# A gated linear attention with a mixture of eight experts: first unit's decay in two interleaved halves, expert rows gathered ahead of weights, range verdict moved into the last expert

## The chip, the cores and the metric

The kernel runs on one core of a Trainium2 chip. The metric is the device time of one execution in microseconds, the median of three runs. A core has a matrix engine (PE, with its weight loads shown apart as PEld), a vector engine (DVE), a scalar engine (ACT), a general-purpose engine (POOL) and a queue engine (SP) that here only starts transfers. Each engine works through its own list of instructions in the order in which they stand there. A profile of one execution gives every instruction with its start, its length and what released it.

## What is computed

The reference has two blocks. The first is a gated linear recurrence with a complex decay for each channel, for 4 batches, 8 heads, 768 steps and 48 channels a head; its output is regrouped into 3072 rows of 384. The second sends every row to the one of eight experts that has the largest logit, and scales the result by the softmax weight of that expert.

```python
mag = np.sqrt(a_re * a_re + a_im * a_im)
scale = np.minimum(mag, 0.999) / (mag + 1e-06)
a_re_n, a_im_n = (a_re * scale, a_im * scale)
for t in range(S):
    new_re = ar * S_re - ai * S_im
    new_im = ar * S_im + ai * S_re
    S_re, S_im = (new_re + kv, new_im)          # kv: outer product of k and v at t
    y[:, :, t] = np.einsum('bhd,bhde->bhe', q[:, :, t], S_re)
...
expert_idx = np.argmax(x @ w_gate, axis=1)
for e in range(E):
    h = np.maximum(x_sorted[lo:hi] @ w1[e], 0.0)
    y_sorted[lo:hi] = h @ w2[e]
return gate_w[:, None] * y
```

## The kernel before

**Attention stage.** The recurrence is computed in chunks of 128 steps. There are 24 chunks (6 blocks of time by 4 batches), and two of them, of two neighbouring batches, make a unit: 12 units, u = 0 to 11, with tiles of 128 partitions by 768 columns (`W`). For each unit SP loads ar and ai (the real and imaginary decay), q, k and v, of 384 KB each (`load`, line 257). The tiles ar, q and k have two buffers, ai and v three. Then:

- `decay_steps` (277) makes the logarithm of the decay's size, in the tile A, and the tangent of its angle, in ai. ACT and DVE alternate: Ln of ar; Exp, DVE product with ai (289), Square; Ln, DVE add (294); Exp, DVE minimum and subtract (299). R holds what passes from one to the other.
- `decay_angle` (303) makes the angle by Arctan on ACT, for which another table of functions has to be loaded, and later units pass the angle at the end of their time block on by small transfers that POOL starts (309, 318, with a DVE addition in c at 315).
- `decay_sums` (327) and `angle_sums` (356) are prefix sums over the 128 steps by products with a triangular matrix on PE (csl for the size, cst for the angle), then Exp on ACT (E and Ei) and a reduction to one turn on DVE.
- `rotation` (379) makes cosine and sine; `decayed` (387) and `rotated` (395) multiply them into q and k, which gives the tiles Q and K.
- `scores` (481) transposes Q and K on PE (tp), copies them out (qt, kt), multiplies them (at) and masks the result on DVE (am); dk is the chunk's contribution to the state. `outputs` (510) adds the two parts of y, updates the state G, transposes y back and computes the routing logits.

The loop over u (587) works on the decay of unit u + 1, on the angles of unit u, and on scores and outputs of unit u - 1. A scheduler puts the instructions of each engine into order when the kernel is built, so an edit in one place can move instructions elsewhere; some are tied to one another by `queue`, which all ACT functions of the decay are. `busy` (248) puts idle products of the identity matrix with itself on PE at the start, whose results nobody reads: 30 before the first sums and 28 after those of the first unit.

**Routing and experts.** `choose` and `route` find each row's expert and place; POOL scatters the rows with an indirect transfer to the DRAM tile `xs`, where each expert has 448 places. `gather` (550) loads the rows of one expert, in an order of experts that is computed on the chip, in four copies to the tile sq (two buffers) and one or two small ones to gi (gate and row number). `turn` (671) transposes sq to xt by DVE in three instructions, `expert` (704) forms hps = w1 times xt, in eight groups of three products, with relu to ht in turns on DVE and ACT, and then yps = ht times w2, whose tiles of 128 rows DVE scales by the gate to y and POOL scatters to the output. The first expert is done in two parts, of 256 and 192 rows. Its second part gathers its rows after the attention stage; then come `load_w(1)` and, at the start of that part (811), the gather of the second expert. Weights have two sets of buffers, so those of expert e + 2 are loaded behind expert e (824).

**Range check.** The fast formulas hold for decays within a range. From the second to the seventh expert, ACT and POOL check two of twelve slices of ar and ai each (`range_check`, 760, between hps and yps of the expert), and leave sums in `bad`. `verdict` (779) adds them up on DVE, lets PE sum over partitions (`bp`, 798), and writes the flag that decides, at the end of the kernel, if slower code has to be run. It stands after the seventh expert (829). With the inputs here, the flag is zero and the slow code isn't run.

Of the kernel before, what the change touches and what calls it, by code (L numbers as in the profile page):

```python
# [10 lines left out]
FP = mybir.dt.float32  # L11
# [3 lines left out]
OP = mybir.AluOpType  # L15
# [5 lines left out]
P = 128  # L21
# [16 lines left out]
def kernel(  # L38
# [189 lines left out]
    def act(**kw):  # L228

        ins = nc.scalar.activation(**kw)  # L230
        if "act" in T:
            queue(ins, T["act"])
        T["act"] = ins
# [20 lines left out]
                queue(w, m)  # L254
            m = w

    def load(u, names):
        for nm, src in names:
            if nm == "v":
                t = vbuf[u % 3][:, :, :, 0:D]  # L260
                T[nm, u] = vbuf[u % 3]
            else:
                t = ld.tile([P, U, H, D], FP, tag=nm, name=nm, bufs=3 if nm == "ai" else 2)
                T[nm, u] = t.rearrange("p c h d -> p (c h d)")
            s, b = divmod(u * U, B)
            T["ld"] = nc.sync.dma_start(
                out=t.rearrange("p c h d -> p (c h) d"),
                in_=src[b : b + U, :, s * P : (s + 1) * P, :].rearrange("b h t d -> t (b h) d"),
            )

    def load_a(u):
        load(u, (("ar", a_re), ("ai", a_im)))
# [1 line left out]
    def load_qkv(u):  # L274
        load(u, (("q", q), ("k", k), ("v", v)))

    def decay_steps(u):

        ar, ai = T["ar", u], T["ai", u]
        A = un.tile([P, W], FP, tag="A", name="A")  # L280
        R = un.tile([P, W], FP, tag="R", name="R", bufs=1)
        T["L", u], T["th", u] = A, ai

        def s0():
            act(out=A, in_=ar, func=AF.Ln)

        def s1():
            act(out=R, in_=A, func=AF.Exp, scale=-1.0)
            nc.vector.tensor_tensor(out=ai, in0=ai, in1=R, op=OP.mult)
            act(out=R, in_=ai, func=AF.Square)  # L290

        def s2():
            act(out=R, in_=R, func=AF.Ln, bias=1.0)
            nc.vector.scalar_tensor_tensor(out=A, in0=A, scalar=2.0, in1=R, op0=OP.mult, op1=OP.add)

        def s3():

            act(out=R, in_=A, func=AF.Exp, scale=-0.5, bias=ln2e6)
            nc.vector.scalar_tensor_tensor(out=A, in0=A, scalar=LN_CAP2, in1=R, op0=OP.min, op1=OP.subtract)

        return [s0, s1, s2, s3]

    def decay_angle(u):

# [51 lines left out]
    def angle_sums(u, c):  # L356

        if c == 0:
            for nm in ("f", "fa"):
                T[nm, u] = un.tile([P, W], FP, tag=nm, name=nm, bufs=1)  # L360
        sl = slice(c * DM, (c + 1) * DM)
        f = T["f", u][:, sl]
        cs = sums("cst", u, c)
        m = mm(cs, tri_turn, T["th", u][:, sl])
        if u == 0 and c == 1:
            busy(m, 28)
        r = ch.tile([P, DM], FP, tag="r", name="r")
        nc.vector.tensor_scalar(out=r, in0=cs, scalar1=MAGIC, scalar2=MAGIC, op0=OP.add, op1=OP.subtract)
        nc.vector.tensor_tensor(out=f, in0=cs, in1=r, op=OP.subtract)
        if c == U - 1:  # L370
            f, fa = T["f", u], T["fa", u]
            nc.vector.tensor_scalar(
                out=fa.bitcast(I32), in0=f.bitcast(I32), scalar1=0x7FFFFFFF, scalar2=None, op0=OP.bitwise_and
            )
            if (u + 1) * U <= NT - B:
                T["fl", u] = un.tile([96, 8], FP, tag="fl", name="fl", bufs=3)
                nc.gpsimd.dma_start(out=T["fl", u], in_=f[P - 1 : P].rearrange("o (p j) -> o p j", j=8))
# [172 lines left out]
    def gather(e, s, sizes):  # L550

        n, w = len(sizes), sum(sizes)
        f, nb = w // P, -(-w // TB)
        sq = gp.tile([P, nb, KD * TB], FP, tag="sq", padded_shape=[P, CAP // TB, KD * TB], name="sq")
        gi = gp.tile([P, n, 2], FP, tag="gi", padded_shape=[P, CT, 2], name="gi", bufs=3)
        rows = xs[0:NS].rearrange("(e s) c -> e s c", s=CAP)[ds(ex[e], 1), s : s + nb * TB]
        for a in range(QB):  # L560
            x = rows[:, :, a * KD * TB : (a + 1) * KD * TB]
            nc.sync.dma_start(out=sq[a * TB : (a + 1) * TB], in_=x.rearrange("o (b j) c -> j (o b) c", j=TB))
        nc.sync.dma_start(out=gi[:, :f], in_=rows[:, : f * P, DM:].rearrange("o (i p) c -> p (o i) c", p=P))
        if f < n:
            nc.sync.dma_start(out=gi[0 : w - f * P, f], in_=rows[:, f * P : w, DM:].rearrange("o p c -> (o p) c"))
        return sq, gi

    load_a(0)
    load_qkv(0)
    for z in range(2):  # L570
        nc.sync.dma_start(
            out=wg[z * DP : z * DP + D, :, 0:E],
            in_=w_gate.rearrange("(i z d) e -> z d i e", z=2, d=D)[z],
        )
    load_a(1)
    busy(None, 30)
    table("natural_log_exp_and_others")
    for f in decay_steps(0):
        f()
    table("trig_and_small")  # L580
    decay_angle(0)
# [5 lines left out]
    for u in range(NU + 1):  # L587
        if 0 < u < NU:
            load_qkv(u)
        for i in range(NS // (P * BL)):  # L590
            if 2 + i * 2 // (NS // (P * BL)) == u:
                blank(i)

        if u < NU:
            steps = decay_steps(u + 1) if u + 1 < NU else []
            own = [lambda c=c: decay_sums(u, c) for c in range(U)]
            steps = steps[:1] + (own + steps[1:] if u == 0 else own[:1] + steps[1:2] + own[1:] + steps[2:])
            table("natural_log_exp_and_others")
            for i, f in enumerate(steps):
                f()  # L600
                if i == 1:
                    carry_angle(u)
            for f in T.pop("chosen", []):
                f()
            for c in range(U):
                angle_sums(u, c)
            table("trig_and_small")
            rotation(u)
            if u + 1 < NU:
                decay_angle(u + 1)  # L610
            if u == NU - 1:
                while T["put"]:
                    place()
                experts_at(range(1), True)
                load_w(0, range(KD + KF // 2))
                own0 = gather(0, 0, [P] * (FIRST // P))
        if u < NU:
            place()
        for f in T.pop("route", []):
            T["put"] += f()  # L620
        for c in range(U):
            g = (u - 1) * U + c
            if g >= 0:
                scores(g)
            if u < NU:
                decayed(u, c)
            if g > 0:
                outputs(g - 1)

            n = {NT - GR: GR, NT - U: U}.get(g)  # L630
            if n:
                if n == GR:
                    queue(table("natural_log_exp_and_others"), T["copied"])
                choose(g - n, n)()
                T["put"] += route(g - n, n)
                while T["put"]:
                    place()
        for _ in range(2 if u >= NU - 2 else 1):
            place()
        if u > 2 and u % 2 and u < NU - 1:  # L640

            j = (u - 3) * U
            T["chosen"] = [choose(j, GR)]
            T["route"] = [lambda j=j: route(j, GR)]
        if u + 2 < NU:
            load_a(u + 2)
# [10 lines left out]
    def tiles(n):  # L657
        return [P] * (n // P) + [n % P] * (n % P > 0)

    rest0 = gather(0, FIRST, tiles(CAPS[0] - FIRST))  # L660
    experts_at(range(1, E), False)
    load_w(1)
    xp = ctx.enter_context(tc.tile_pool(name="xp", bufs=2))
    hp = ctx.enter_context(tc.tile_pool(name="hp", bufs=2))
# [134 lines left out]
        nc.vector.tensor_copy(out=flag, in_=bp)  # L799

    flag = const([1, 2], "flag", I32)
    parts = [(0, [P] * (FIRST // P), own0), (0, tiles(CAPS[0] - FIRST), rest0)]
    xt = turn(parts[0][1], own0[0])
    for e in range(E):
        if e in (1, E - 1):
# [1 line left out]
            T["drain"] = queue(nc.gpsimd.drain(), T["out"])  # L807
        while parts and parts[0][0] == e:
            sizes, (sq, gi) = parts.pop(0)[1:]
            if not parts and e + 1 < E:  # L810
                parts.append((e + 1, tiles(CAPS[e + 1]), gather(e + 1, 0, tiles(CAPS[e + 1]))))
            last = not parts or parts[0][0] > e
            todo = []
            if last and 1 <= e < E - 1:
                todo = [lambda b, i=i: range_check(i, b) for i in range(NC) if i % (E - 2) == e - 1]

            def ahead():
                if parts:
                    T["xt"] = turn(parts[0][1], parts[0][2][0])

            expert(sizes, xt, *W_T[e], gi, todo, ahead)
            xt = T["xt"]
        if e + 2 < E:
            load_w(e + 2)
        for i in range(NC):
            if i % (E - 2) == e:
                range_load(i)
        if e == E - 2:
            verdict()


    TS = 16
# [85 lines left out]
    def others():  # L918
        with tc.tile_pool(name="mo", bufs=1) as mo:
# [8 lines left out]
            with tc.For_i(0, E, 1) as ev:  # L928
# [8 lines left out]
                with tc.For_i(0, NT, 1) as jv:  # L937
                    nc.vector.tensor_copy(out=fi, in_=fr[:, ds(jv, 1)])
                    xg = gp.tile([P, XW], FP, tag="sq", padded_shape=[P, KD * CAP], name="xg")
                    gi = gp.tile([P, 1, 2], FP, tag="gi", padded_shape=[P, CT, 2], name="gi", bufs=3)  # L940
                    nc.gpsimd.indirect_dma_start(
                        out=xg,
                        out_offset=None,
# [42 lines left out]
```

## Time and profile before

| what | value |
| --- | --- |
| median of 3 runs | 563.52 us (563.12 to 565.4) |
| span of the profiled execution | 561.2 us |
| PE busy | 530.6 us, 95% |
| DVE busy | 271.4 us, 48% |
| ACT busy | 278.0 us, 50% |
| POOL busy | 130.2 us, 23% |
| first transpose of Q on PE | at 27.81 us |
| first product of an expert | at 283.51 us |
| moved by DMA | 79.32 MB |

The span is a little shorter than the measured time, which holds the start and end of the program too. A busy PE is not one at its peak: the lengths of its instructions overlap, and its clock can be lower than full, which the profile gives as granted clock (1.00 is full, 0.50 half). In a timeline each line has the start and the length in us, the engine, the line of the kernel, the operation, the tiles written and read, and, where the engine stood idle before the instruction, for how long and what released it. Idle time of an engine costs nothing unless PE waits for that engine in the end.

### The profile page before, as it was taken

The numbers are of one execution on the slowest core, as the hardware profiler recorded it, in microseconds if no ns is written. First come the engines' busy times: TensorE is split into PE (matmuls) and PEld (weight loads), VectorE is DVE, ScalarE is ACT, GpSimd is POOL, SyncE is SP. The second block draws the span as 40 slices with busy tenths as digits, with TensorE's granted clock in tenths as the row PEclk, the third lists the DMA queues.
The fourth block names the chain that finished last, engine by engine and source line by source line (L and its number), as shares of the span: only waits on it lengthen the run. The fifth ranks groups of instructions, "written<-read, shape, count | busy, mean of one in ns | idle before, by whom it ended". The sixth has DMA issues, their size and how long they took to land.

```text
span 561.2 us, 8750 instructions
## 1 busy us (share of the span) xinstructions
PE 530.6 (95%) x3294; PEld 367.8 (66%) x3294; DVE 271.4 (48%) x637; ACT 278.0 (50%) x468; POOL 130.2 (23%) x148
## 2 busy tenths in 40 slices
PE   6699999989999999999999899999999999999895
PEld 6587677768778778777776545555555555565462
DVE  2567788688888888878442122112222131210310
ACT  5777967857787687745310105326152341616100
POOL 2101111131141140210221003406143250604201
PEclk9879999989999999999999999999999999999998
DMA  9999995937575543460117893373945718390001
GB/s 158 182 220 260 246 158 66 171 83 119 108 140 95 107 93 58 98 231 12 48 60 234 231 266 127 110 204 130 280 133 178 231 48 263 126 293 15 26 2 42
DMA packets 163534, 79.32 MB, mean 141 GB/s; under 512 B 144864, under 2 KB 156829, under 8 KB 162587
## 3 DMA queue, kind: packets, MB, share of 16 engines
q1 hardware_dynamic: 158619, 69.04, 53.8%
q0 software_dynamic: 4864, 9.63, 5.1%
q8 instruction: 28, 0.46, 0.3%
q14 instruction: 23, 0.19, 0.1%
HBM read 63.30 MB, written 15.46 MB: 140 GB/s over the span
## 4 chain that ended last, share of the span: by engine, by line
PE 73%; ACT 3%; DVE 3%; issue 2%; DMA 2%; POOL 1%; POOLq 0%; DVEq 0%; ACTq 0%
PE hps L81 24%; PE yps L81 21%; PE y L81 7%; PE at L81 6%; PE tp L492 5%; PE dk L81 3%; PE csl L81 2%; PE cst L81 2%; PE tpx L542 2%; DMA c<-ai 2%; PE lt L81 1%; ACT L242 1%; PE lp L81 1%; POOL cai L774 1%; POOL cs L771 1%
## 5 line engine op out<-in xcount | busy, mean ns | idle before, releaser
L81 PE MATMUL hps<-xt,w1t 128*128 128x256 f32 (+8 forms) x432 | 133.9, 469 | 2.3 <-DVE xt L679 2.3
L81 PE MATMUL yps<-w2t,ht 128*128 128x384 f32 (+6 forms) x464 | 135.0, 487 | 0.0
L81 PEld LDWEIGHTS hps<-xt,w1t 128*128 128x128 f32 x432 | 80.0, 190 | 54.3 <-issue 24.8
L81 PEld LDWEIGHTS yps<-w2t,ht 128*128 128x128 f32 (+6 forms) x464 | 75.9, 177 | 57.0 <-issue 7.1
L713 ACT ACTIVATE ht<-hps 128x256 f32<-128x256 f32 (+8 forms) x36 | 17.0, 472 | 132.2 <-PE hps L81 131.3
L730 DVE TENSOR_SCALAR y<-yps,gi 128x384 f32<-128x384 f32 (+2 forms) x24 | 14.8, 616 | 106.6 <-PE yps L81 106.6
L717 DVE TENSOR_SCALAR ht<-hps 128x256 f32<-128x256 f32 (+8 forms) x36 | 19.2, 533 | 83.6 <-PE hps L81 83.5
L81 PE MATMUL at<-qt,kt 96*128 96x128 f32 x384 | 54.9, 284 | 3.4 <-DVE kt L84 2.7
L81 PEld LDWEIGHTS at<-qt,kt 96*128 96x128 f32 x384 | 49.2, 195 | 10.4 <-DVE kt L84 3.2
L81 PE MATMUL y<-am,v 128*64 128x128 f32 x384 | 51.0, 286 | 0.6 <-DVE am L500 0.5
L693 POOL DMA_INDIRECT out_dram<-y,gi x29 | 28.2, 972 | 93.0 <-DVE y L730 42.8
L470 POOL DMA_INDIRECT xs<-x,slot x24 | 26.2, 1090 | 89.2 <-DMA xs<-x,slot 29.1
L81 PE MATMUL y<-qt,G 96*64 96x128 f32 x320 | 46.0, 281 | 0.7 <-DVE G L537 0.7
L771 POOL TENSOR_TENSOR cs<-cs,cw 128x768 f32<-128x768 f32 x12 | 21.7, 1807 | 87.1 <-ACT cw L767 87.1
L500 DVE TENSOR_TENSOR am<-at,tri 128x512 f32<-128x512 f32 x48 | 33.0, 687 | 14.7 <-PE at L81 14.6
L81 PEld LDWEIGHTS y<-am,v 128*64 128x64 f32 x384 | 33.1, 137 | 9.6 <-issue 8.0
L492 PE MATMUL tp<-ident,Q 128*96 128x128 f32 x192 | 33.5, 285 | 2.1 <-DVE Q L398 1.7
L81 PEld LDWEIGHTS y<-qt,G 96*64 96x64 f32 x320 | 32.6, 137 | 4.4 <-issue 2.7
L242 ACT ACT_TABLE_LOAD x27 | 34.6, 1283 | 1.2 <-PEq L972 0.8
L84 ACT COPY qt<-tp 96x512 f32<-96x512 f32 x48 | 27.8, 581 | 14.0 <-PE tp L492 13.9
L81 PEld LDWEIGHTS dk<-v,K 128*96 128x96 f32 x320 | 31.1, 170 | 3.2 <-issue 1.1
L81 PE MATMUL dk<-v,K 128*96 128x48 f32 x320 | 31.7, 252 | 0.8 <-DVE t L530 0.8
(140 smaller groups left out, 745.9 us busy)
## 6 DMA issues: line engine op xcount, KB each, us to landing
w1t<-in_moe_w_dram SPq DMA_DIRECT2D x7, 1536.0 KB, 6.6
w2t<-in_moe_w_dram SPq DMA_DIRECT2D x7, 1536.0 KB, 7.2
xs<-zrow SPq DMA_DIRECT2D x7, 772.0 KB, 8.7
ar<-in_a_re_dram SPq DMA_DIRECT2D x12, 384.0 KB, 5.9
ai<-in_a_im_dram SPq DMA_DIRECT2D x12, 384.0 KB, 6.6
q<-in_q_dram SPq DMA_DIRECT2D x12, 384.0 KB, 5.8
k<-in_k_dram SPq DMA_DIRECT2D x12, 384.0 KB, 6.2
v<-in_v_dram SPq DMA_DIRECT2D x12, 384.0 KB, 5.1
```

Source lines behind the costliest of these rows:

```text
L81: return nc.tensor.matmul(o, lhsT=lhsT, rhs=rhs, start=start, stop=stop, skip_group_check=True)
L84: (nc.scalar.copy if i % 2 else nc.vector.tensor_copy)(out=o, in_=in_)
L242: ins = nc.scalar.preload_act_table_set(name)
L470: pool(nc.gpsimd.indirect_dma_start(out=xs[:, :], out_offset=bass.IndirectOffsetOnAxis(ap=to[:, i : i + 1], axis=0), in_=x[:, i], in_offse ...
L492: nc.tensor.transpose(out=tp[0:DD, j], in_=X[:, hg * 4 + j], identity=ident)
L500: nc.vector.tensor_tensor(out=am, in0=at, in1=bc(tri, 1, 4), op=OP.mult)
L542: nc.tensor.transpose(out=tp[:, i].rearrange("p z d -> p (z d)"), in_=xt[:, i], identity=ident)
L693: T["out"] = nc.gpsimd.indirect_dma_start(out=out, out_offset=bass.IndirectOffsetOnAxis(ap=idx, axis=0), in_=y[0:m], in_offset=None, bound ...
L713: relu = nc.scalar.activation(out=ht[:, f], in_=ps, func=AF.Relu)
L717: nc.vector.tensor_scalar(out=ht[:, f], in0=ps, scalar1=0.0, scalar2=None, op0=OP.max)
L730: nc.vector.tensor_scalar(out=y[0:m], in0=ps[0:m], scalar1=gate, scalar2=None, op0=OP.mult)
L771: nc.gpsimd.tensor_tensor(out=s, in0=s, in1=w, op=OP.add)
```

## The change

It has three parts. In the first unit the loads of ar and ai are cut into two halves (one batch each), and the steps of the decay are done half by half in turns, so that one half's ACT function can be worked on during the other half's DVE operation; the second unit's ar is loaded ahead of the first unit's q and k, its ai ahead of the first unit's v. There are 28 idle products before the first sums and 38 after. For all later units the steps are the same as before, but in five pieces in place of four, which the loop interleaves a little differently.

Secondly, the rows of the second expert are gathered ahead of its weights, and those of every later expert one expert sooner, ahead of the weights that are loaded behind the expert at work; gi has four buffers in place of three. The third part calls the verdict within the last expert, between its two products, in place of after the seventh expert.

```diff
-    def load(u, names):
-        for nm, src in names:
...
+    def load(u, names, cuts=1):
+
+        s, b = divmod(u * U, B)
+        n = U // cuts
+        for c in range(0, U, n):
+            for nm, src in names:
...
+                T["ld"] = nc.sync.dma_start(
+                    out=t[:, c : c + n].rearrange("p c h d -> p (c h) d"),
+                    in_=src[b + c : b + c + n, :, s * P : (s + 1) * P, :].rearrange("b h t d -> t (b h) d"),
+                )
...
-    def decay_steps(u):
+    def decay_steps(u, cuts=1):
...
+        def steps(sl):
+            ar, ai, a, r = [t[:, sl] for t in (T["ar", u], T["ai", u], A, R)]
...
+            return [s0, s1, s2, s3, s4]
+
+        w = W // cuts
+        return [steps(slice(i * w, i * w + w)) for i in range(cuts)]
...
-            busy(m, 28)
+            busy(m, 38)
...
-        gi = gp.tile([P, n, 2], FP, tag="gi", padded_shape=[P, CT, 2], name="gi", bufs=3)
+        gi = gp.tile([P, n, 2], FP, tag="gi", padded_shape=[P, CT, 2], name="gi", bufs=4)
...
-    load_a(0)
-    load_qkv(0)
+    load(0, (("ar", a_re), ("ai", a_im)), 2)
+    load(1, (("ar", a_re),))
+    load(0, (("q", q), ("k", k)))
+    load(1, (("ai", a_im),))
+    load(0, (("v", v),))
...
-    load_a(1)
-    busy(None, 30)
+    busy(None, 28)
     table("natural_log_exp_and_others")
-    for f in decay_steps(0):
+    first, second = decay_steps(0, 2)
+
+    for f in first[:2] + second[:1] + first[2:3] + second[1:2] + first[3:4] + second[2:4] + first[4:] + second[4:]:
         f()
...
-            steps = steps[:1] + (own + steps[1:] if u == 0 else own[:1] + steps[1:2] + own[1:] + steps[2:])
+            if u == 0:
+                steps = steps[:2] + own + steps[2:]
+            else:
+                steps = steps[:1] + own[:1] + steps[1:3] + own[1:] + steps[3:]
...
-    rest0 = gather(0, FIRST, tiles(CAPS[0] - FIRST))
+    parts = [(0, [P] * (FIRST // P), own0)]
+
+    def part(e, s=0):
+
+        sizes = tiles(CAPS[e] - s)
+        parts.append((e, sizes, gather(e, s, sizes)))
+
+    part(0, FIRST)
     experts_at(range(1, E), False)
+    part(1)
     load_w(1)
...
-            if not parts and e + 1 < E:
-                parts.append((e + 1, tiles(CAPS[e + 1]), gather(e + 1, 0, tiles(CAPS[e + 1]))))
             last = not parts or parts[0][0] > e
+            if last and e + 2 < E:
+                part(e + 2)
...
             def ahead():
                 if parts:
                     T["xt"] = turn(parts[0][1], parts[0][2][0])
+                else:
+                    verdict()
...
-        if e == E - 2:
-            verdict()
```

More of the change, by code (lines that the diff above doesn't have):

```diff
@@ L255, in busy @@
             m = w
-    def load(u, names):
-        for nm, src in names:
[L259 to L269, printed above, removed]
+    def load(u, names, cuts=1):
[3 more added lines that the diff above has]
+            for nm, src in names:
+                if nm == "v":
+                    T[nm, u] = vbuf[u % 3]
+                elif c == 0:
+                    t = ld.tile([P, U, H, D], FP, tag=nm, name=nm, bufs=3 if nm == "ai" else 2)
+                    T[nm, u] = t.rearrange("p c h d -> p (c h d)")
+                t = vbuf[u % 3][:, :, :, 0:D] if nm == "v" else T[nm, u].rearrange("p (c h d) -> p c h d", h=H, d=D)
+                T["ld"] = nc.sync.dma_start(
+                    out=t[:, c : c + n].rearrange("p c h d -> p (c h) d"),
+                    in_=src[b + c : b + c + n, :, s * P : (s + 1) * P, :].rearrange("b h t d -> t (b h) d"),
+                )
     def load_a(u):
@@ L275, in load_qkv, with s0, s1, s2 @@
         load(u, (("q", q), ("k", k), ("v", v)))
-    def decay_steps(u):
-        ar, ai = T["ar", u], T["ai", u]
+    def decay_steps(u, cuts=1):
         A = un.tile([P, W], FP, tag="A", name="A")
         R = un.tile([P, W], FP, tag="R", name="R", bufs=1)
[L282 to L301, printed above, removed]
+        T["L", u], T["th", u] = A, T["ai", u]
+        def steps(sl):
+            ar, ai, a, r = [t[:, sl] for t in (T["ar", u], T["ai", u], A, R)]
+            def s0():
+                act(out=a, in_=ar, func=AF.Ln)
+            def s1():
+                act(out=r, in_=a, func=AF.Exp, scale=-1.0)
+                nc.vector.tensor_tensor(out=ai, in0=ai, in1=r, op=OP.mult)
+            def s2():
+                act(out=r, in_=ai, func=AF.Square)
+            def s3():
+                act(out=r, in_=r, func=AF.Ln, bias=1.0)
+                nc.vector.scalar_tensor_tensor(out=a, in0=a, scalar=2.0, in1=r, op0=OP.mult, op1=OP.add)
+            def s4():
+                act(out=r, in_=a, func=AF.Exp, scale=-0.5, bias=ln2e6)
+                nc.vector.scalar_tensor_tensor(out=a, in0=a, scalar=LN_CAP2, in1=r, op0=OP.min, op1=OP.subtract)
+            return [s0, s1, s2, s3, s4]
+        w = W // cuts
+        return [steps(slice(i * w, i * w + w)) for i in range(cuts)]
     def decay_angle(u):
@@ L594 @@
         if u < NU:
-            steps = decay_steps(u + 1) if u + 1 < NU else []
+            steps = decay_steps(u + 1)[0] if u + 1 < NU else []
             own = [lambda c=c: decay_sums(u, c) for c in range(U)]
-            steps = steps[:1] + (own + steps[1:] if u == 0 else own[:1] + steps[1:2] + own[1:] + steps[2:])
+            if u == 0:
+                steps = steps[:2] + own + steps[2:]
+            else:
+                steps = steps[:1] + own[:1] + steps[1:3] + own[1:] + steps[3:]
             table("natural_log_exp_and_others")
@@ L801 @@
     flag = const([1, 2], "flag", I32)
-    parts = [(0, [P] * (FIRST // P), own0), (0, tiles(CAPS[0] - FIRST), rest0)]
     xt = turn(parts[0][1], own0[0])
@@ L939, in others @@
                     xg = gp.tile([P, XW], FP, tag="sq", padded_shape=[P, KD * CAP], name="xg")
-                    gi = gp.tile([P, 1, 2], FP, tag="gi", padded_shape=[P, CT, 2], name="gi", bufs=3)
+                    gi = gp.tile([P, 1, 2], FP, tag="gi", padded_shape=[P, CT, 2], name="gi", bufs=4)
                     nc.gpsimd.indirect_dma_start(
```

## The prediction, made before the changed kernel was run

> **What bounds the kernel now.** I read the busy table first: PE has work for 530.6 of 561.2 us (95%), ACT and DVE for half, so the time can fall only where PE stands still or runs slowly. The next view is the list of what PE waited for, whole run: engine, tile and releaser, then us in total, times, longest.
>
> ```profile
> PE csl L81 <- DVE A L299: 5.9, 2, 2.9
> PE at L81 <- DVE kt L84: 2.7, 2, 2.4
> PE hps L81 <- DVE xt L679: 2.3, 1, 2.3
> PE bp L81 <- DVE two L796: 2.3, 1, 2.3
> ```
>
> The first line is the start, where the first two units' decays are made; the second lies in the attention stage; the last two are single stops in the expert stage. Then the stages, by windows: us, busy time of PE, PEld, DVE, ACT and POOL, granted PE clock, DMA share, GB/s.
>
> ```profile
> 10.00:12.80 2.80, 0.00 (x0) 0.00 (x1) 1.74 (x2) 1.96 (x2) 0.00 (x0) 1.00 1.42 159
> 12.80:22.00 9.20, 9.10 (x64) 7.84 (x64) 5.32 (x11) 7.17 (x11) 2.15 (x3) 1.00 1.35 178
> 22.00:25.00 3.00, 0.17 (x1) 0.17 (x2) 1.77 (x2) 2.13 (x2) 0.00 (x0) 1.00 1.09 197
> 25.00:35.50 10.50, 9.06 (x40) 6.90 (x41) 6.05 (x8) 7.65 (x13) 0.00 (x0) 0.51 1.08 180
> 35.50:284.00 248.50, 237.28 (x2232) 188.60 (x2231) 192.28 (x452) 174.78 (x300) 50.25 (x68) 0.99 0.63 126
> ```
>
> PE stands for nearly 3 us twice, and after the second time it works 10 us at half clock (0.51). From 35.5 to 284 it is busy 95%: what arrives earlier at the start should end earlier too.
>
> The DVE timeline at the first expert stop (start, us, then idle before and releaser):
>
> ```profile
> 318.23 0.62 DVE L730 TENSOR_SCALAR y<-yps,gi 128x384 f32<-128x384 f32 x1 [5.78 <-PE yps L81]
> 321.53 0.55 DVE L741 TENSOR_TENSOR y<-yps,y 64x384 f32<-64x384 f32 x1 [2.69 <-ACT y L739]
> 322.12 0.41 DVE L742 TENSOR_SCALAR y<-y,gi 64x384 f32<-64x384 f32 x1
> 322.45 2.08 DVE L679 STREAM_TRANSPOSE xt<-sq 128x448 f32<-128x448 f32 x3
> ```
>
> The second expert's transposes have no idle time of their own: they stand behind two instructions that wait for the last product of the first expert, which PE ended at 320.92. PE goes on at 323.26, after the first of the three transposes. At the second stop:
>
> ```profile
> 521.46 0.18 DVE L789 TENSOR_SCALAR bad<-bad 128x24 f32<-128x24 f32 x1 [8.93 <-ACT cai L767]
> 521.63 1.83 DVE L679 STREAM_TRANSPOSE xt<-sq 128x384 f32<-128x384 f32 x3
> 523.88 0.17 DVE L791 TENSOR_REDUCE two<-bad 128x1 f32<-128x24 f32 x1
> ```
>
> DVE waits 8.93 us for the range check on ACT; behind it stand the last expert's transposes and the sums for the PE product bp, which is ahead of the last expert's products. PE, free at 522.2, starts bp at 524.49.
>
> [...]Here the first ar (384 KB) is issued at 0.75, ACT starts on it at 4.92, and DVE starts on ai, issued next, at 7.08: 2.16 us for 384 KB, so 4.17 - 2.16 = 2.01 us fixed[...]. [...] the idle time from 22 leads to 0.51, that from 9.9 to 12.8 does not[...]. [...]
>
> **Part 1, the start.** Halves of the first unit's ar and ai (192 KB, 1.08 us each) land at 3.84, 4.92, 6.00 and 7.08; then whole tensors 2.16 us apart: second unit's ar 9.2, q 11.4, k 13.6, second unit's ai 15.7, v 17.9. No bytes are added. No row shows a half-length ACTIVATE from SBUF. From below it is the 128x384 one from PSUM, 0.47[...]. I take 0.47, a step of 0.50 where it waits for the one before and 0.37 where not[...]. A half DVE operation is 0.55 (row Qe).
> Chain: ACT Ln 3.84, Exp to 4.81; DVE product 4.95 to 5.50; ACT Ln of half two 6.00 (its landing), Square, Exp to 7.2; DVE product of half two to 7.8; Ln(1+) of half one to 7.6; DVE add to 8.3; Square and Ln of half two to 8.8; DVE add, behind 0.65 us of small set-up work that stands in its queue, to 9.45; the two Exp to 10.0; DVE ends at 10.1 and 10.6. Before: Exp to 11.76, DVE to 12.75. So ACT is 1.77 us earlier, angle and two table loads (1.28 each) included: at the second unit's ar at 13.44, not 15.21. There before waits 0.77 more for the load (15.98); now it landed at 9.2. That makes **2.5 us**. DVE then has ai at 15.7 (before 19.11) and the product Q, before at 26.80, can start at 24.3; its inputs q and k, landing by 13.6, are needed at 16.6. v lands late but is read first by dk, after 26.
> The idle products: 28 take 6.41 us (0.229 each), 38 take 8.7. From 13.7, when the angle sums are done, they reach 22.4; the second unit's csl can go at 22.65. PE then has pauses of 0.3 and, before Q at 25.3, 1.9 us in place of 2.9 and 1.4. That is below the stop of 2.9 that kept full clock once, so I expect no half clock. What it was worth: the first product at stood at 34.17, when its input had been ready at 31.6: **2.6 us** behind. ACT lost 2.81 us there to PE too, so it can follow. From below this is 0 (clock falls anyway). The 30 idle products ahead become 28, hidden: their end (9.3) is before csl is due (10.2).
>
> **Part 2, rows ahead.** In the changed order on DVE the second expert's transposes stand behind the copy at 318.23, not behind those of 321.53 and 322.12, so PE need not stop at 320.92: **2.3 us**, if the rows are there by 318.85. Their gather, issued at 300.88 to 313 beside the weights, is now issued right after the rest of the first expert's rows: four row copies from about 299.6, 4.9 us as the later gathers take, to 304.5, and two small ones to 306.6. With 9 to 12 us to landing (table of issues) the rows are there by 313.5 to 316.5, and sooner without 3 MB ahead of them. Price: the second expert's weights are issued 7 us later, at 306.6; with 6.6 and 7.2 us to landing each and the second queued they are there by 321 at the latest, w1 by 314, needed at 320.9 (w2 at 339). Later gathers gain an expert's length, and I cost them at nothing: they are behind nothing that ends late before either. A fourth gi buffer costs only space.
>
> **Part 3, the verdict.** In the changed order DVE still has bad behind the range check, with the sums and two copies y behind it, but the transposes are well ahead, and bp stands after the last expert's hps. The copies wait until 522; their PSUM bank is next written at 537. The next ht copy is due at 524.1 (hps 1.9 us after 522.2), DVE is free at 523.3. The DVE sums end at 522.8, bp is reached at 537, and its 0.1 us stays. Gain **2.3 us**.
>
> **Sum:** 563.5 - 2.5 - 2.6 - 2.3 - 2.3 = 553.8; I say 553.6, as the order around one stop (below) looks a little better.
>
> **Rivals.** (a) All four, 553.6: 50%. (b) The start gives 2.5 but the clock still halves, or ACT (18.9 of 21 us busy from 50 to 71) takes that gain back: 556.4, 18%. (c) All of the start is lost at a later fixed wait: at 113 PE stands 2.4 us for kt, which stands on DVE behind c, waiting 3.92 us for a small DMA; the queue of that DMA is busy (share 1.2 to 1.3 from 100 to 113). Were it bound to the load traffic, PE would only wait longer there: 558.9, 12%. Against: DMA share falls to 0.6 after, so the loads follow the compute. (d) That stop goes: in the changed order kt stands ahead of the ai product and Qe (0.95 + 0.55) there; with it goes the clock of 0.64 from 116 to 120, 1.4 us: 553.6 - 2.4 - 1.4 = 549.8, 14%. (e) Slower: the attention stage is interleaved anew on PE, DVE and ACT; four new stops of 2.4 us with 1.4 us of half clock each (4 x 3.8 = 15) outweigh 9.9: 569, 6%. The even pace of the stage, 42.1 us for each two units, speaks against it.
>
> **Numbers.** Range 549.5 to 559.5: from (d) to (c), with 0.6 us for the half-length ACTIVATE and small shifts; left out are (e) and the outer edges. Faster (under 560.7) are (a) to (d) but a little: 0.91; same 0.04; slower 0.05.
>
> **What would show it.** ACT's second-unit Ln near 13.5; the first Q transposes near 25.3 and at near 29; clock 1.0 from 25 to 35; no PE wait for xt or two; the first expert product near 278, 5 us earlier than 283.5; PE idle from there to the end under 1 us. Wrong would be: a clock of 0.5 at 25, a new PE wait for DVE above 2 us in 40 to 280, a wait for rows or w1 of the second expert.

## The result, and the profile after

The changed kernel takes 557.59 us (median of 4 runs, 556.42 to 558.87), the kernel before 563.32 us in the same comparison; the ratio is 0.9896, with a 95% interval of 0.9857 to 0.9935. It is faster, by 5.8 us, within the range of the prediction and 4 us above its figure. The experiments show that it came about in another way than forecast: the term of the experts holds, that of the start has the wrong sign in the end, and one that the prediction set to zero is the largest. That the time lies in the forecast range is therefore luck: two large errors nearly cancel.

The list of what PE waited for in the changed kernel (engine, tile, releaser; us in total, times, longest):

```profile
PE tp L504 <- DVE kt L84: 3.1, 2, 2.6
PE cst L81 <- issue: 3.0, 1, 3.0
PE tpx L554 <- ACT xt L551: 2.1, 3, 0.7
PE tp L504 <- DVE Q L410: 1.8, 1, 1.8
```

The waits for A at the start, for xt and for two are gone from it, as the change meant. At the head of the list stand two waits that have grown: kt for a transpose (0.4 us before), and cst for "issue" (0.9 us before), by which the profile means that it shows nothing that PE waited for.

The start, in the timeline (start, us, engine, line, operation, tiles, and the idle time before with its releaser):

```profile
13.14 0.84 ACT L230 ACTIVATE A<-ar 128x768 f32<-128x768 f32 x1
...
24.50 0.64 PE L504 MATMUL tp<-ident,Q 128*96 128x128 f32 x4 [1.75 <-DVE Q L410]
...
28.83 0.39 PE L81 MATMUL at<-qt,kt 96*128 96x128 f32 x2
```

ACT begins the second unit at 13.14 (before 15.98), Q is transposed at 24.50 (before 27.81), and the first product at stands 5.3 us ahead of its 34.17 before. The windows (us; busy time of PE, PEld, DVE, ACT, POOL; clock, DMA share, GB/s) show that PE kept full clock:

```profile
25.00:35.50 10.50, 9.13 (x74) 7.17 (x72) 9.31 (x15) 9.65 (x16) 1.12 (x2) 1.00 1.29 202
35.50:284.00 248.50, 237.50 (x2192) 186.88 (x2191) 187.59 (x445) 169.67 (x291) 50.62 (x65) 0.98 0.56 123
```

Yet the first product of an expert starts at 284.06, before at 283.51. All of the 5.3 us is lost within the attention stage, in which PE is as busy as before. PE stands for over 2 us at two places there. The first stop, in the timeline of 46 to 49 us:

```profile
47.56 0.16 DVE L327 SCALAR_TENSOR_TENSOR c<-fl,c 96x8 f32<-96x8 f32 x1 [3.57 <-DMA c<-ai]
47.65 0.68 DVE L84 COPY kt<-tp 96x512 f32<-96x512 f32 x1
...
48.38 0.73 PE L504 MATMUL tp<-ident,Q 128*96 128x128 f32 x3 [2.58 <-DVE kt L84]
```

DVE waits 3.57 us for a small transfer of angles (96 by 8 numbers); behind it stands kt, and PE waits for kt. The transfer was issued at 41.30, behind loads of ar and ai of 384 KB each (issued at 37.62 and 38.95), and landed 6.2 us later. It is the pattern that the prediction saw at 113 us; there the transfer now lands 3.6 us after its issue, and PE waits 0.5 us for kt. The second stop, in the timeline around 240 us:

```profile
237.55 0.55 POOL L330 DMA_DIRECT2D ai<-c  x1
...
240.78 0.39 PE L81 MATMUL y<-am,v 128*64 128x128 f32 x4
...
244.20 0.98 PE L81 MATMUL cst<-ai,tri_turn 128*128 128x384 f32 x1 [3.04 <-issue]
```

cst reads the tile ai, into which the small transfer issued at 237.55 writes the last angles. The first expert's weights, 3 MB, had been issued from 233.35 on. PE stands 3.04 us and then works at half clock:

```profile
240.00:244.00 4.00, 1.17 (x16) 0.74 (x13) 1.18 (x4) 1.22 (x2) 0.00 (x0) 0.89 0.96 351
244.00:250.00 6.00, 5.80 (x18) 4.18 (x19) 2.81 (x6) 0.58 (x1) 2.02 (x2) 0.50 0.19 71
```

In the expert stage the change did what it was made for. The timeline of the first expert stop, and of the second:

```profile
318.78 0.62 DVE L757 TENSOR_SCALAR y<-yps,gi 128x384 f32<-128x384 f32 x1 [5.78 <-PE yps L81]
...
319.31 2.11 DVE L706 STREAM_TRANSPOSE xt<-sq 128x448 f32<-128x448 f32 x3
...
321.40 1.40 PE L81 MATMUL hps<-xt,w1t 128*128 128x448 f32 x3
...
322.08 0.55 DVE L768 TENSOR_TENSOR y<-yps,y 64x384 f32<-64x384 f32 x1 [0.66 <-ACT y L766]
```

```profile
519.59 0.18 DVE L816 TENSOR_SCALAR bad<-bad 128x24 f32<-128x24 f32 x1 [8.92 <-ACT cai L794]
...
520.17 2.02 PE L81 MATMUL hps<-xt,w1t 128*128 128x368 f32 x6
```

The transposes now follow the copy y at 318.78 directly, and PE goes on at 321.40 with no idle time. At the second stop DVE still waits 8.92 us for the range check, but nothing that PE needs stands behind it. From the first expert product to the end it is 557.0 - 284.06 = 272.9 us; before it was 561.2 - 283.51 = 277.7. So the experts gave 4.8 us, the attention stage nothing.

### The profile page after: what moved, and what is told of

Its sections match the earlier page's. It is cut to its first block, busy times and chain, and to the rows that moved or that the text cites. A ratio compares the mean times of both kernels' runs of the same rounds, so it can differ in the third digit from the quotient of the medians.

```text
span 557.0 us, 8781 instructions
## 1 busy us (share of the span) xinstructions
PE 535.4 (96%) x3310; PEld 370.5 (67%) x3310; DVE 271.3 (49%) x640; ACT 279.3 (50%) x473; POOL 132.5 (24%) x148
## 4 chain that ended last, share of the span: by engine, by line
PE 79%; issue 3%; DMA 2%; DVE 2%; ACT 2%; POOL 0%; POOLq 0%; DVEq 0%; ACTq 0%
PE yps L81 24%; PE hps L81 24%; PE y L81 8%; PE at L81 6%; PE tp L504 6%; PE dk L81 4%; PE cst L81 3%; DMA c<-ai 2%; PE csl L81 2%; PE tpx L554 1%; PE lt L81 1%; PE lp L81 1%; DVE am L512 0%; ACT xt L551 0%; PE mt L362 0%
## 5 line engine op out<-in xcount | busy, mean ns | idle before, releaser
L482 POOL DMA_INDIRECT xs<-x,slot x24 | 28.3, 1179 | 94.0 <-DMA xs<-x,slot 34.3
L81 PE MATMUL y<-am,v 128*64 128x128 f32 x384 | 49.8, 285 | 0.7 <-DVE am L512 0.7
L81 PEld LDWEIGHTS y<-am,v 128*64 128x64 f32 x384 | 31.4, 135 | 10.6 <-issue 7.5
L504 PE MATMUL tp<-ident,Q 128*96 128x128 f32 x192 | 32.1, 281 | 4.9 <-DVE kt L84 3.1
L81 PEld LDWEIGHTS y<-qt,G 96*64 96x64 f32 x320 | 30.9, 136 | 5.0 <-issue 4.0
L504 PE MATMUL tp<-ident,K 128*96 128x128 f32 x192 | 31.4, 280 | 0.2 <-DVE K L410 0.2
L81 PEld LDWEIGHTS dk<-v,K 128*96 128x96 f32 x320 | 29.5, 165 | 2.5 <-issue 2.0
```

The lines of the kernel that those rows point to most:

```text
L81: return nc.tensor.matmul(o, lhsT=lhsT, rhs=rhs, start=start, stop=stop, skip_group_check=True)
L482: pool(nc.gpsimd.indirect_dma_start(out=xs[:, :], out_offset=bass.IndirectOffsetOnAxis(ap=to[:, i : i + 1], axis=0), in_=x[:, i], in_offse ...
L504: nc.tensor.transpose(out=tp[0:DD, j], in_=X[:, hg * 4 + j], identity=ident)
```

## The experiments

Times are set against runs of the kernel before in the same comparison (medians 563.5 to 564.8). A ratio of 0.01 is 5.6 us. Where a stage is compared, the mark is the first expert product.

**Is the second stop the weights' fault?** Only SP's order changes: the first expert's weights are issued behind its first rows.

```diff
-                load_w(0, range(KD + KF // 2))
                 own0 = gather(0, 0, [P] * (FIRST // P))
+                load_w(0, range(KD + KF // 2))
```

> The changed kernel with one edit: the first expert's weights (3 MB) are issued behind the first gather of rows, not ahead of it, so that they start at about 252 us, not at 233. Only SP's list of transfers differs; PE, DVE, ACT and POOL have the same order. Theory A (the lead of the start is lost where PE waits for the small angle transfer of the last unit, which stands behind those weights in the DMA queues): the stop of PE before cst at 241 us (3.0) and the half clock after it go, the angle transfer ai<-c lands within 4 us, the first expert product comes 4 to 6 us earlier (278 to 280), time 552 to 553.5. Rival B (the new order of the attention stage itself is slower and that stop is only where it shows): the stop may go, but PE stands elsewhere, first expert product within 1 us of 284, time 557 to 558. Rival C: the weights come too late; a new stop at the first hps or gather; time above 558.

Measured: 553.33 us, ratio 0.9814 (0.9777 to 0.9851), first expert product at 277.88. Its timeline:

```profile
237.15 0.54 POOL L330 DMA_DIRECT2D ai<-c  x1
...
240.70 0.91 PE L81 MATMUL cst<-ai,tri_turn 128*128 128x384 f32 x2
...
248.28 0.89 SPq L212 DMA_DIRECT2D w1t<-in_moe_w_dram  x2
```

The transfer of angles is issued 0.4 us earlier than in the changed kernel; cst starts 3.55 us after it without waiting, where it stood until 6.65 us after it. The profile also gives the time from the issue of this one transfer to its landing, in the changed kernel and then here:

```profile
DMA to landing us min/median/max: 6.6/6.6/6.6
```

```profile
DMA to landing us min/median/max: 1.9/1.9/1.9
```

PE's list of waits for this kernel has no wait above 2.1 us in total. So the wait called "issue" is that for a small transfer which lands 6.6 us after its issue behind 3 MB of weights, and 1.9 us after it without them. In ratio the edit is worth 0.0082, 4.6 us, half clock included.

**What do rows and verdict give without the new start?** The kernel before, with the second and third part of the change and the old start.

> Parts two and three alone: the kernel before, with the second expert's rows ahead of its weights, later rows one expert sooner, and the verdict in the last expert. The order of the attention stage on every engine is that of before. Both theories on the attention stage leave the stops of 2.3 and 2.3 us before the second and the last expert gone: first expert product at 283.5 as before, PE without idle time from there, time 4.6 us below before, about 558.7. If the whole gain of the change comes from here, this is within 1 us of the changed kernel; if the start brought something in the end, the changed kernel is faster than this one.

Measured: 553.97 us, ratio 0.9801 (0.9764 to 0.9839), first expert product at 279.55. This was not foreseen: it is faster than the changed kernel, and its attention stage, in which each engine's order is that of before, ends 4 us earlier than before. Something in the two parts acts on the attention stage. One thing could: with four gi buffers in place of three, 32 bytes more in each partition lie ahead of the attention's tiles. In the built kernels the load tiles start at 105,888 before, an odd multiple of 32, and now at 105,920, a multiple of 64.

**Is it the place of the tiles?** Three kernels. The kernel before with the fourth gi buffer alone:

```diff
-name="gi", bufs=3)
+name="gi", bufs=4)
```

> The kernel before with the gi buffers raised from 3 to 4 and nothing else; the order on every engine is that of before. It only moves the attention's load tiles by 32 bytes in each partition, from an odd multiple of 32 to a multiple of 64. Theory A, the start address of the 192-byte pieces sets the load's pace: the loads of 384 KB are issued every 1.7 us in place of 2.05 in the first 25 us, the first ar lands near 4.6 (before 4.92), the stop near 113 shrinks as it did with the old start, first expert product near 279.5, and the time falls by 4 us to 559.5 (ratio near 0.992 or below). Theory B, a place in SBUF is only space, and the old start with the rows and the verdict gained its 4 us of attention by something else: 563.5 to 564.5, ratio 1.000, loads at 2.05.

The changed kernel with an unused tile of 32 bytes, which moves the load tiles on, to an odd multiple of 32 again:

```diff
     zrow = const([P, XW], "zrow")
+    const([P, 8], "pad")
```

> The changed kernel with an unused tile of 32 bytes among the constants, which moves the load tiles back to an odd multiple of 32; the order on every engine is that of the changed kernel. Theory A (start address of the pieces): issue of 384 KB loads back to 2.05 us, about 1 us lost in the first 10 us, Ln of the second unit later than 13.14, and 559.5 to 562 (the changed kernel has 557.6). Theory B (only space): 557.6 within 1, same pace of loads.

And the kernel before, three gi buffers, with such a tile ahead of the v buffers:

```diff
+    const([P, 8], "pad")
     vbuf = [const([P, U, H, DP], f"v{i}") for i in range(3)]
```

> The kernel before with one unused tile of 32 bytes ahead of the v buffers and nothing else: v then stands at a multiple of 256 and the load tiles at a multiple of 64, as with the fourth gi buffer. Theory A (start address of the pieces): at least what the fourth gi buffer gave, 558.0, and 0 to 2 us more for v: 556 to 558. Theory B (the fourth gi buffer helps as a buffer, not by its place): 563.5.

| kernel | load tiles start at | time, us | ratio (95%) |
| --- | --- | --- | --- |
| before with four gi buffers | multiple of 64 | 558.04 | 0.9885 (0.984 to 0.993) |
| before with one tile of 32 bytes | multiple of 64 | 559.88 | 0.9925 (0.9902 to 0.9947) |
| changed kernel | multiple of 64 | 557.59 | 0.9896 (0.9857 to 0.9935) |
| changed with one tile of 32 bytes | odd multiple of 32 | 563.71 | 1.0001 (0.9983 to 1.002) |

The place counts, as theory A had it: 32 bytes are worth 4 to 6.5 us, in both directions, and the changed kernel with its load tiles at an odd multiple of 32 is no faster than the kernel before. In all three, each engine's order is that of its counterpart. The issue of loads in the timeline of SP's queue, before and then with four gi buffers:

```profile
4.53 2.06 SPq L266 DMA_DIRECT2D k<-in_k_dram  x1
6.63 2.05 SPq L266 DMA_DIRECT2D v<-in_v_dram  x1
```

```profile
4.30 1.76 SPq L266 DMA_DIRECT2D k<-in_k_dram  x1
6.10 1.75 SPq L266 DMA_DIRECT2D v<-in_v_dram  x1
```

These loads of 384 KB hold the queue 1.76 and 1.75 us in place of 2.06 and 2.05; in the changed kernel moved on, the loads of q and k issued at 29.48 and 31.61 hold it 2.04 and 2.00, the same two in the changed kernel (at 26.29 and 28.22) 1.84 and 1.64. The v tiles stand at the same address with three gi buffers and with four, so the place of a load's own tile is not what alone sets its time in the queue. The windows say the same of the pace: GB/s (the last column) before, and with four gi buffers:

```profile
2.00:10.00 8.00, 7.87 (x60) 7.67 (x58) 1.98 (x8) 3.41 (x5) 1.77 (x12) 1.00 1.36 194
10.00:25.00 15.00, 9.27 (x65) 8.02 (x66) 8.83 (x14) 11.26 (x14) 2.15 (x3) 1.00 1.31 178
```

```profile
2.00:10.00 8.00, 8.00 (x51) 8.00 (x50) 2.54 (x8) 3.40 (x5) 1.77 (x12) 1.00 1.25 220
10.00:25.00 15.00, 11.19 (x77) 9.13 (x75) 8.27 (x14) 12.57 (x16) 2.15 (x3) 0.98 1.19 198
```

The start gains 1.3 us by it (Q's transposes at 26.48, before 27.81). The rest comes later: the longest wait of at for kt falls from 2.4 to 1.4 us, the clock from 110 to 122 us stays at 1.00 (before 0.86), and the first expert product is at 279.42, 4.1 us earlier. The tiles behind the load tiles moved too, so that the runs do not show the loads as the only carrier.

Why the place counts was not shown. The pieces of these loads are 192 bytes. With four gi buffers the pace rose by 13% from 2 to 10 us (194 to 220 GB/s) and by 11% from 10 to 25 us (178 to 198), and the queue time of the two loads above fell by 15%. The kernel with the one tile also shows a way in which such a gain is lost. Its times range from 557.54 to 568.23 us; the profiled execution, of 564.74, has this wait, 3.7 us of it near 60 us in the attention stage, with half clock behind it (0.50 from 60 to 64 us):

```profile
PE cst L81 <- issue: 4.5, 2, 3.7
```

**Do the v buffers matter too?** They start at an odd multiple of 32 too. Two tiles of 32 bytes put v and the load tiles on multiples of 256. This was done on two bases: the old start with rows, verdict and the weights behind the rows, and the changed kernel with the weights behind the rows.

```diff
+    const([P, 8], "pad0")
     vbuf = [const([P, U, H, DP], f"v{i}") for i in range(3)]
...
+    const([P, 8], "pad1")
     zrow = const([P, XW], "zrow")
```

> The old start with rows, verdict and four gi buffers (553.97 before), and the first expert's weights issued behind its first rows instead of ahead of them. If the weights ahead delay the last small angle transfer also here, a wait of PE near 238 goes and the time is 550 to 552, first expert product at 276 to 278. If with the old start that transfer has landed before the weights are issued, 554 within 0.7 and first expert product at 279.5.

> As the run with the old start and the weights after the rows, and two unused tiles of 32 bytes: one puts the three v buffers on a multiple of 256 (they stood at 224 of 256[...]), the other keeps the load tiles on a multiple of 64 (now 0 of 256 instead of 192). Theory A: the load of v takes less than that of q and k in issue time, 1.4 to 1.7 us, and the time falls by 0 to 2 us, since loads bind only at the start and at single stops. Theory B: no change, within 0.7.

> The changed kernel with the first expert's weights behind its first rows (553.33) and two unused tiles of 32 bytes: v on a multiple of 256, load tiles on a multiple of 256. If quicker loads help the new start too (its v is the last of the first unit's loads and is needed late, its next units' loads are not), the load of v is issued in 1.2 to 1.5 us and the time is 550 to 552; if they bind nothing any more, 553.3 within 0.8. With the old start the same step left 552.66 against 552.34.

| kernel | time, us (range) | ratio (95%) |
| --- | --- | --- |
| old start, weights behind rows | 552.34 (550.93 to 553.54) | 0.9781 (0.9738 to 0.9823) |
| the same, v aligned | 552.66 (549.57 to 557.46) | 0.9805 (0.9753 to 0.9857) |
| changed, weights behind rows, v aligned | 551.32 (550.89 to 551.71) | 0.9785 (0.9758 to 0.9812) |

With the old start the two tiles bring nothing. With the new one the time is 2 us below the same kernel without them (553.33), but the intervals of the ratios overlap, so a gain is not shown. The first load of v holds the queue 1.51 us in the third of these kernels (1.62 in the changed kernel), and 1.71 in the kernel before with one tile of 32 bytes, where v stands on a multiple of 256 too (1.75 with four gi buffers, where it does not). All three beat both kernels. The new start, with the weights behind the rows, is neither better nor worse than the old (0.9814 against 0.9781, intervals overlap). With the old start, moving the weights behind the rows brought 1.1 us (0.9801 to 0.9781), within the intervals.

**Does the clock at the start matter?** The changed kernel with 28 idle products behind the first sums in place of 38 (`busy(m, 28)`).

> The changed kernel with 28 idle products after the first unit's sums in place of 38. They end 2.3 us earlier, at about 19.7 us, and PE then has pauses of about 2.1 and 1.7 us round csl. If the clock is what I took it for: it falls to half at about 23 to 25 us for some 10 us and the product at comes near 31.4, not at 28.8. Theory A (what is gained at the start is taken at the next wait for an angle transfer): time as the changed kernel within 1.5 us. If the start's clock carries through: 2.6 us slower. The order of the attention stage changes with this edit too (58 places on PE), which can move the time by some us either way.

Measured: 556.82 us, ratio 0.9861 (0.9825 to 0.9897), the same as with 38. Its clock from 25 to 35.5 was 0.61 and at came at 31.10, 2.3 us after that of the changed kernel; the first expert product came at 284.06, as in the changed kernel. The order of the attention stage on PE changed with this edit too, so it is not a test of the clock alone. What the clock had taken at the start, the later waits did not need to take. Full clock was no property of the 38 products either: in five other profiled kernels that have the new start and 38 of them, the clock from 25 to 35.5 was 0.51 to 0.67.

**What does the start do alone?** The kernel before with four gi buffers and the first part of the change.

> The kernel before with four gi buffers (558.04) and the start in halves, rows and verdict as before. Theory A, the start costs more than it brings, by the stops near 48 and 241 and the half clock behind them, 557.59 - 553.97 = 3.6 us: 561.7, first expert product near 284, both stops expert of 2.3 us kept. Theory B, the start is harmful only together with the rows (other order of the scheduler): 558.0 or less. As the prediction had it: 558.0 - 5.1 = 552.9.

Measured: 562.63 us, ratio 0.9983 (0.9958 to 1.0008): beside the 0.9885 of four gi buffers alone, the start costs 0.0098, 5.5 us. Its list of waits has the same entry as the changed kernel:

```profile
PE cst L81 <- issue: 3.1, 1, 3.1
```

**Rows and verdict apart.** The changed kernel with the verdict back after the seventh expert, and the kernel before with four gi buffers and only the verdict moved; the edit in both is

```diff
+                else:
+                    verdict()
...
-        if e == E - 2:
-            verdict()
```

taken back in the first and made in the second.

> The changed kernel with part three undone alone: the verdict after the seventh expert. Only bp and the copy of its result move, to before the last expert's products. My prediction had part three at 2.3 us: then PE stops 2.3 us before bp and the time is 560. The trace of the changed kernel says less: DVE has the sums ready at 520.77 and PE is free at 520.17, since the last expert's transposes are no longer ahead of the sums; then PE stops 0.6 us and the time is within 0.8 us of the changed kernel.

> The kernel before with four gi buffers (558.04) and the verdict in the last expert, rows as before, old start. On DVE only the copy of flag moves; the last expert's transposes still stand behind bad, which waits for the range check. Theory A, the last expert's stop has two causes, either of which is enough: PE need not wait for two any more, but waits some 0.5 us for the first transpose in its place, so 1.8 us are gained: 556.2, and the first expert stop of 2.3 us near 320 stays. Theory B, as predicted, the verdict holds the whole 2.3: 555.7. Theory C, it holds nothing without the earlier rows: 558.0.

Measured: 557.54 us, ratio 0.9878 (0.9843 to 0.9912), and 557.27 us, ratio 0.9893 (0.9868 to 0.9919). Neither differs from its base by more than the intervals. The stage is a finer measure: from the first expert product to the end the four combinations take 277.8 us (neither, 557.2 - 279.42), 275.8 (verdict alone, 554.2 - 278.44), 273.5 (rows alone, 555.8 - 282.30) and 272.9 (both). With rows alone, PE's wait for two is

```profile
PE bp L81 <- DVE two L823: 0.5, 1, 0.5
```

The second stop had two things behind bad on DVE, the transposes and the sums. Early rows take the transposes away from there and leave 0.5 us of 2.3; the verdict takes away the sums and leaves some 0.2. Either is nearly enough. Two more profiled kernels have neither, the start alone and the one with one tile of 32 bytes: there the stage takes 279.3 and 279.4 us. The first expert stop is 2.3 us long in all of them. The longest product hps takes 1112 ns with the start alone and 954 with the one tile, where it is 643 in the kernel before and with the verdict alone. So the stage is 1.5 us longer (279.3 against 277.8) where single products are slower; that the stop makes them so was not shown.

## Why the prediction was right and where it was wrong

In ratios, with what the prediction had for each:

| step | runs compared | ratio | us of 563.5 | predicted |
| --- | --- | --- | --- | --- |
| 32 bytes (fourth gi buffer) | before, four gi buffers | 1 to 0.9885 | -6.5 | 0 |
| rows and verdict | four gi buffers, old start | 0.9885 to 0.9801 | -4.7 | -4.6 |
| start | old start, changed | 0.9801 to 0.9896 | +5.4 | -5.1 |
| sum | | 0.9896 | -5.9 | -9.7 |

The other way round gives the same: without the 32 bytes the change stands at 1.0001, the start alone adds 5.5, rows and verdict behind it take 4.9. Each ratio is known to 1 to 2.5 us, so a step to 2 to 3.5.

- **"A fourth gi buffer costs only space"** is the step that failed most. It cost nothing and brought the largest gain of the change, for a reason that has nothing to do with gi. The tiles' place stood nowhere in the sum: 0 us predicted, 6.5 measured. Without it, the forecast of faster would have been wrong, so that this forecast came true by luck.
- **Part 1, the 2.5 us**, is right where it was measured. Without the 32 bytes the second unit's Ln on ACT stands at 13.70 and Q's transposes at 25.15, 2.66 us earlier than before. The landings were the author's estimate from the first two loads of before: 3.84 and 6.00 for the two halves of ar, where their Ln began at 3.87 and 5.95 in that run. Half-length functions took 0.51 to 0.52 us; the 0.47 was that of the same shape from PSUM.
- **Part 1, the clock (2.6)**, happened in the profile of the changed kernel and in no other with the new start. That pauses below 2.9 us keep full clock was the author's estimate from one stop of before (9.9 to 12.8 us). PE's pause ahead of Q was 1.75 us in the profile with full clock, and 1.75 or 1.76 in the five with 0.51 to 0.67.
- **"What arrives earlier at the start should end earlier too"** is where part 1 fell. The step read 95% busy as a stage without fixed times. Small transfers of angles hold it at single places: behind bulk transfers they landed 6.2 us after their issue at 48 us and 6.6 at 241, where 3.6 near 108 us and, with the weights behind the rows, 1.9 at the last of them were measured. How much of the lead was lost where can be read from the first mask product am (on DVE) of a unit, set against the run with the old start and the tiles in the same places: the changed kernel is 4.8 us ahead in the first unit, 2.5 in the second, level in the ninth (199.54 against 199.53), and 4.5 behind at the first expert product. The stop at 48 us takes no more than full clock had given: the run with the weights behind the rows had no full clock there, waits 0.6 us at most for kt, and has am of the second unit at 52.18, the changed kernel at 52.26. The stop at 241 us, with its half clock, comes after the lead is gone, and turns it into a loss. Where the 2.5 us between the second and the ninth unit go stays open; with the weights behind the rows in both, the new start's lead shrinks there too, from 2.0 to 0.7, while PE has no long wait. At the last of the small transfers the old start, with the same weights ahead, had PE there 4.24 us after the transfer's issue and going on at 5.06; the changed kernel had it there at 3.61 and going on at 6.65. The order dealt anew by the scheduler explains 0.6 us of that; why the transfer itself landed 1.6 us later stays open. In the stops it is the mechanism of rival (c), at 48 and 241 us instead of 113, and the outcome is larger: not only all of the start is lost, but 5 us more. The reason given against (c), that loads follow the compute, left out the weights, which are issued at a fixed place ahead of the last transfer. With them behind the rows neither a price nor a gain of the start can be told any more.
- **Part 2 and part 3** have the right sum, 4.6 predicted and 4.8 in the stage, and the wrong split: 2.3 each, where rows alone give 4.3, the verdict alone 2.0, and the verdict behind the rows 0.6. The sum of part 2 left out that with the rows early, the last expert's transposes go from the second stop too.
- Rival (d) was right that the stop at 113 goes; its gain does not show at the end of the stage. Of the signs listed, Ln near 13.5, Q near 25.3, at near 29, clock 1.0 from 25 to 35, no wait for xt or two came true; the first expert product near 278 did not, and the new wait for DVE above 2 us, listed under "wrong", was there.

## What to carry to other kernels

Before an edit to pools is costed at nothing, look at where the tiles behind it then start: a buffer of 32 bytes moved them here, and loads in pieces of 192 bytes went from 178 to 198 GB/s. A comparison of two versions with different pools should include one in which only the place is moved. And a lead gained at the start should not be credited at the end of a long stage from a high busy share alone: list the small transfers that PE or DVE waits for, and what bulk transfer is issued just ahead of each.

## What the runs showed of the hardware

- The first unit's loads of k and v, 384 KB each in pieces of 192 bytes, issued one behind the other, took 2.06 and 2.05 us of queue time with the load tiles at an odd multiple of 32, and 1.76 and 1.75 with them at a multiple of 64; the tile of v itself had not moved.
- The small transfer of the last angles landed 1.9 us after its issue with the weights behind the rows, 6.6 us after it with 3 MB of weights ahead in the changed kernel, and 5.1 us after it with the same 3 MB ahead in the kernel before.
- Behind the same 38 idle products, pauses of 0.2 to 1.8 us on PE between 22 and 28 us were followed by a clock of 1.00 from 25 to 35.5 us in one profile and of 0.51 to 0.67 in five others.
- With the same stop of 2.3 us on PE at the second expert's rows, the longest product hps took 643 ns in two profiles, and 954 and 1112 ns in two others.
